# Weight conversions in halves over the steps of the first block, and two copies moved to VectorE

## The chip, the cores and the metric

The kernel runs on one core of one Trainium2 chip. The metric is device microseconds of one launch. Before the change it takes 2700.61 us, the median of 8 runs (2700.15 to 2704.35). A core has five engines that run side by side, each through its own list in order: TensorE (PE; its weight loads are listed as PEld), VectorE (DVE), ScalarE (ACT), GpSimd (POOL) and SyncE (SP), which here issues most DMAs. They wait for each other by semaphores.

## The reference

For 8 sequences of 3008 tokens with 256 channels, a Fourier mixing along the tokens and then a feed-forward layer with hard-swish:

```python
X = np.fft.rfft(x, axis=1)
Y = X * (filt_r + 1j * filt_i)[None]
y = np.fft.irfft(Y, n=3008, axis=1)        # (8, 3008, 256) -> (24064, 256)
h = y @ w_in                               # 256 -> 2048
g = h * np.clip(h + 3.0, 0.0, 6.0) / 6.0
return g @ w_out                           # 2048 -> 256
```

`setup_inputs()` generates the two weights as float64, so the kernel reads them as pairs of 32-bit words and makes float32 of them by itself.

## The kernel before, in words

**Blocks and steps.** The 24064 tokens are 47 blocks of 512. Each block goes through 8 steps, one for each 256 of the 2048 hidden channels; step i of the whole kernel is block i // 8, part p = i % 8. In a step PE multiplies by `w_in[p]` (up), ACT and DVE apply hard-swish, and PE multiplies the step before's result by `w_out[p-1]` (down). The Fourier stages of the following sequence are laid between these products. The order of all instructions is written out by hand: `at(step, function, ...)` puts a call into a plan, the loop over `items` (L925) emits it, and every engine works through its instructions in this order. Within a step, calls of `a_unit`, `b_unit`, `bi_unit` and `n_unit` (the tuple EARLY) come ahead of the down products, all others at the step's end, in the order in which they were planned.

**The first block.** Steps 0 to 7 are block 0, which uses plain products: `plain_up(p)` (L653) writes two PSUM tiles, `al` and `be`, by two matmuls each (L658); `relu` on ACT (L616) and `hswish` on DVE (L621) read each of them and write `g`; `plain_down(p)` (L662, matmuls L669), emitted in step p+1, multiplies `g` by `w_out[p]`. There is one `al` and one `be`, so `plain_up(p+1)` can write them only when `hswish(p)` has read them. Steps from 8 on are block 1 and later: they use seven products in place of eight (`up_1` to `up_5`, L571; `g_sums`; `down`, L647). `plain_down(7)` falls into step 8.

**The conversions.** The weights come in 16 parts of 512 KB: part 2p is `w_in[p]`, part 2p+1 is `w_out[p]`. `w_load` (L260) brings the words of one part into a `bits`, `g` or `xt` tile by a DMA on SP; parts 6, 7 and 10 to 15 share two `bits` tiles, so that part i+2's load waits until part i's words are read. `load_bits` issues the loads that are due. `w_abs` (L266, ACT) takes the upper words' absolute value; `w_conv` (DVE) makes the float32 values by seven instructions: L275, L277, L279, L281, L288, L290, and L293, which writes the whole part into `w_all`, the tile with all weights. Parts 0 to 3 are converted ahead of step 0, parts 4 to 15 in steps 0 to 6 by `convert_one` (one, then two in each of steps 1 to 5, then one), at the end of the step, behind that step's two `hswish` on DVE.

**Sums of weights.** The seven products need sums of the weights' quarters. `w_sums` (L299, POOL) makes three early ones for a part (`late` False) and one late one, which overwrites a quarter and so must come after block 0 has used the part. They are planned from step 6 on; those of parts 14 and 15 begin at step 6.

**First stage of sequence 1.** `a_unit(1, c)`, c = 0 to 7 in steps 2 to 9, transforms slices of `x`: 16 matmuls into two PSUM tiles `psf` (L385), which two ACT copies (L388) bring into the tile `t`; `z_store` sends it to memory on SP's queue. For later sequences there is one copy, and `a_sums` (L394, L395) does the rest on DVE.

**Around it.** `t_sums` (L564, POOL) makes the differences of the activations that the seven products need; `plain_out` (L676, ACT) copies block 0's result out.

Of the kernel before, what the change touches and what calls it, by code (L numbers as in the profile page):

```python
# [38 lines left out]
NB = HC // XC  # L39
# [6 lines left out]
NP = DFF // 256  # L46
# [90 lines left out]
def kernel(  # L137
# [9 lines left out]
    nc = tc.nc  # L147
# [47 lines left out]
    st = {}  # L195
# [38 lines left out]
    def w_part(i):  # L234
        p = i // 2
        if i % 2 == 0:
            cols = ts(p, 256)
            src = moe_w_in[:, cols].bitcast(I32)
            return src.rearrange("(a p) d -> p a d", p=P), w_in[p][:, 0:4, :].rearrange("p (a j) m -> p a (j m)", a=2)
        src = moe_w_out[ts(p, 2 * P), :].bitcast(I32)  # L240
        return src.rearrange("(a p) d -> p a d", p=P), w_out[p][:, 0:4, :].rearrange("p (a j) m -> p a (j m)", a=2)
# [21 lines left out]
    def w_abs(i):  # L263
        words = st["bits", i].rearrange("p (n two) -> p n two", two=2)
        st["high", i] = sp.tile([P, 512], FP32, name="s1")
        nc.scalar.activation(out=st["high", i], in_=words[:, :, 1].bitcast(FP32), func=AXT.Abs)  # L266


    def w_conv(i):
        words = st.pop(("bits", i)).rearrange("p (n two) -> p n two", two=2)  # L270
        lo, hi = words[:, :, 0], words[:, :, 1]
        big, rest = (yp.tile([P, 2, D], FP32, name="y").bitcast(I32).rearrange("p a n -> p (a n)") for j in range(2))
        v = nc.vector
        high = st.pop(("high", i), None)
        v.tensor_scalar(out=big, in0=hi, scalar1=3, scalar2=0x3FFFFFFF,  # L275
                        op0=ALU.logical_shift_left, op1=ALU.bitwise_and)
        v.scalar_tensor_tensor(out=big, in0=hi, scalar=top_c, in1=big,  # L277
                               op0=ALU.bitwise_and, op1=ALU.bitwise_or)
        v.tensor_scalar(out=rest, in0=big, scalar1=23, scalar2=23,  # L279
                        op0=ALU.logical_shift_right, op1=ALU.logical_shift_left)  # L280
        v.tensor_scalar(out=lo, in0=lo, scalar1=9, scalar2=0x3F800000,  # L281
                        op0=ALU.logical_shift_right, op1=ALU.bitwise_or)
        if high is None:
            v.tensor_scalar(out=hi, in0=hi, scalar1=1, scalar2=1,
                            op0=ALU.logical_shift_left, op1=ALU.logical_shift_right)
            high = hi.bitcast(FP32)
        rest, big = rest.bitcast(FP32), big.bitcast(FP32)
        v.scalar_tensor_tensor(out=rest, in0=lo.bitcast(FP32), scalar=1.0, in1=rest,  # L288
                               op0=ALU.subtract, op1=ALU.mult)
        v.scalar_tensor_tensor(out=rest, in0=rest, scalar=2.0 ** -20, in1=big, op0=ALU.mult, op1=ALU.add)  # L290

        two = lambda t: t.rearrange("p (a d) -> p a d", a=2)
        v.scalar_tensor_tensor(out=w_part(i)[1], in0=two(high), scalar=1.125 * 2.0 ** -15, in1=two(rest),  # L293
                               op0=ALU.is_ge, op1=ALU.mult)
# [74 lines left out]
    def bank(b):  # L369
        if b:  # L370
            return psF.tile([P, 512], FP32, name="psf", tag="f")
        st["bank"] = i = (st.get("bank", -1) + 1) % 4
        return psO.tile([P, 2, 2, P], FP32, name="po%d" % i).rearrange("p a u m -> p (a u m)")
# [4 lines left out]
    def a_unit(b, c):  # L378
        xc = xs[:, (b * NB + c) % 3, :, :]
        t = t1p.tile([P, XC // 2, 2, D], FP32, name="t1")  # L380
        ps = [bank(b).rearrange("p (j d) -> p j d", d=D) for h in range(2)]
        for j in range(2):
            for g in range(2):
                for h in range(2):
                    nc.tensor.matmul(ps[h][ts(g, 64), j, :], wa[ds(h * 64, NA), ds((c * XC + 2 * g + j) * 2 * KH, 64)],  # L385
                                     xc[ds(h * 64, NA), 2 * g + j, :], start=True, stop=True)
        for h in range(2 if b == 1 else 1):
            nc.scalar.activation(out=t[:, :, h, :], in_=ps[h], func=AXT.Copy)  # L388
        st["t1", b, c] = t, ps[1]


    def a_sums(b, c):
        t, ps = st["t1", b, c]
        nc.vector.tensor_tensor(out=t[:, :, 1, :], in0=t[:, :, 0, :], in1=ps, op=ALU.subtract)  # L394
        nc.vector.tensor_tensor(out=t[:, :, 0, :], in0=t[:, :, 0, :], in1=ps, op=ALU.add)  # L395

# [100 lines left out]
    for b in range(B):  # L497
        j = 0
        while j < HC:
            n = 1 if b == 0 and j == NJ else min(NJ, HC - j)  # L500
# [229 lines left out]


    EARLY = (a_unit, b_unit, bi_unit, n_unit)

    def at(step, fn, *a):
        plan.setdefault((step, fn in EARLY), []).append((fn, a))

    with tc.manual_schedule():
# [16 lines left out]
        def load_bits(most):  # L754
            nonlocal loaded
            while loaded < most and w_before(loaded) < done:
                w_load(loaded, nc.sync)
                loaded += 1

        def convert(n):  # L760
            nonlocal done
            for i in range(n):
                w_conv(done)
                done += 1


        def convert_one():
            nonlocal done
            w_abs(done)
            w_conv(done)  # L770
            done += 1
            load_bits(NCONV)

# [2 lines left out]
        ps = psU.tile([P, 512], FP32, name="al")  # L776
# [12 lines left out]
        for j in range(0, HC, 4):  # L789
            a0_unit(j)  # L790
            keep_warm({4: 2, 12: 2, 20: 1}.get(j, 0))
            convert(j == 4)
# [34 lines left out]
        for c in range(2):  # L827
            x_load(1, c)
            load_bits(7 + c)
        w_abs(3)  # L830
        convert(3)

        def wai_load():
# [3 lines left out]
        at(0, bi_unit, 0, NU - 2)  # L837
        at(0, g_store, 0, NU - 2)

        for i, s in enumerate((0, 1, 1, 2, 2, 3, 3, 4, 4, 5, 5, 6)):  # L840
            at(s, convert_one)

        for i in range(2):
            at(6, w_sums, 2 * NP - 2 + i, False)
        for p in range(NP):
            for i in range(2):
                if p < NP - 1:
                    at(p + 6, w_sums, 2 * p + i, False)
                at(p + 6, w_sums, 2 * p + i, True)

        at(0, wai_load)
        at(2, x_load, 1, 2)
# [31 lines left out]
        def places(n):  # L884
            if n == 1:
                return (list(range(2, NB + 2)), [12, 13, 15, 18, 19, 20, 22, 23, 26, 27, 28, 30],
                        [14, 15, 16, 19, 21, 22, 24, 25, 27, 29, 30, 31], [16, 21, 24, 29, 31, 32])
            k = first[n] * NP
            a_at = [k - 7 * NP + i for i in (2, 4, 7, 9, 11, 13, 14, 15)]
            f_at, y_at, bi_at = ([k - (5 - 2 * r) * NP + i for r in range(2) for i in p]  # L890
                                 for p in ((2, 3, 6, 7, 12, 13), (4, 5, 10, 11, 14, 15), (8, 14, 17)))
            return a_at, f_at, y_at, bi_at

        prev = None
        for n in range(1, B):
            a_at, f_at, y_at, bi_at = places(n)
            for c, s in enumerate(a_at):
                at(s, a_unit, n, c)
                if n > 1:
                    at(s, a_sums, n, c)  # L900
                at(s, z_store, n, c, nc.sync if n == 1 else nc.gpsimd)
                if c >= 3:
                    at(max(a_at[c - 3], s - 6), x_load, n, c)
                elif n > 1:
                    at(max(prev[c + NB - 3], s - 6), x_load, n, c)
            for c in range(NT):
                s = f_at[2 * (c - TB) + (n == 1)] + 1 if c >= TB else a_at[-1] + 1
                at(s, t2_load, n, c)
                s = f_at[2 * (c - FB) + 1] + 1 if c >= FB else a_at[-1 if n > 1 else 3] + 1
                at(s, table_load, n, c)  # L910
            for i in range(NU):
                if i % 2 == 0 or n == 1:
                    at(f_at[i], b_unit, n, i)
                if i % 2 == 0:
                    at(bi_at[i // 2], bi_unit, n, i)
                    at(bi_at[i // 2], g_store, n, i)
                at(y_at[i], y_unit, n, i)
            for i in range(NU):
                at(f_at[i], f_unit, n, i)
            prev = a_at  # L920
# [4 lines left out]
        for i in range(len(items) + 1):  # L925
            up = i < len(items)
            k, p = items[min(i, len(items) - 1)]
# [54 lines left out]
        k, v, add = NBLK - 1, nc.vector.tensor_tensor, ALU.add  # L982
# [37 lines left out]
```

## Time and profile before

| | |
|---|---|
| median of 8 runs | 2700.61 us |
| profiled execution | 2700.89 us |
| its span, first to last instruction | 2699.1 us |
| first `plain_up` on PE (step 0) | 67.85 us |
| start of step 8 (block 1) on PE | 135.54 us |
| last matmul's end | 2688.07 us |

Times in the trace are microseconds from the span's start. In a line of an engine's work in order of time stand: start, length, engine, line of the kernel, operation, output <- inputs, shapes, the number of instructions run together, and in brackets the idle time of the engine just before with what ended it. Adjacent instructions of an engine overlap by some hundredths to tenths of a microsecond, so I take differences of starts where a chain is summed. A line of the waits holds who waited for whom, the total, how often, and the longest. A line of a stretch holds its bounds and length, busy time and number of instructions of PE, PEld, DVE, ACT and POOL, the granted clock of TensorE (1.00 is full), the DMA share and GB/s.

### The profile page before, as it was taken

The page shows a single profiled execution, that of the slowest core. Times are in us where ns is not written, and L with a number is a line of the kernel's source. Part 1 is how long each engine was busy: PE and PEld are TensorE (multiplying, and loading weights), DVE is VectorE, ACT ScalarE, POOL GpSimd, SP SyncE. Part 2 cuts the span into 40 slices and gives each one's busy share as a digit, 9 for nine tenths or more (in the row PEclk, how much of TensorE's full clock was granted, in tenths as well). Part 3 has the DMA queues.
Part 4 walks back from the last instruction along what each step waited for, and adds up shares of the span by engine and source line. Part 5 has one row for each costly group of instructions (what it writes and reads, how often), then busy time and mean ns, then how long its engine had stood idle before and what let it go on. Part 6 is the DMA issues. An engine that isn't in the chain of part 4 may idle for free.

```text
span 2699.1 us, 48891 instructions
## 1 busy us (share of the span) xinstructions
PE 2675.2 (99%) x18846; PEld 2365.8 (88%) x18846; DVE 2020.5 (75%) x3503; ACT 1306.4 (48%) x2614; POOL 365.7 (14%) x598
## 2 busy tenths in 40 slices
PE   8999999999999999999999999999999999999998
PEld 6588898888988889888888888988888888899997
DVE  7968867787677776787767877677776778766665
ACT  3444444445444444454544545445444454445443
POOL 2141011001210012101121011211112111000000
PEclk9999999999999999999999999999999999999999
DMA  8732133211332113311133111331123321110000
GB/s 236 218 94 71 46 89 99 69 35 42 92 99 63 35 47 95 99 55 37 47 97 96 55 39 52 89 96 55 39 55 89 94 59 36 42 31 18 18 9 17
DMA packets 106598, 185.89 MB, mean 69 GB/s; under 512 B 23609, under 2 KB 66297, under 8 KB 106049
## 3 DMA queue, kind: packets, MB, share of 16 engines
q1 hardware_dynamic: 88607, 138.05, 18.3%
q0 software_dynamic: 17152, 44.22, 6.2%
q8 instruction: 149, 2.44, 0.4%
q14 instruction: 84, 0.69, 0.1%
q10 hardware_dynamic: 606, 0.49, 0.1%
HBM read 110.74 MB, written 71.93 MB: 68 GB/s over the span
## 4 chain that ended last, share of the span: by engine, by line
PE 96%; DVE 2%; DMA 1%; issue 0%; ACT 0%; POOL 0%; POOLq 0%; DVEq 0%; SPq 0%
PE po L647 43%; PE al L571 24%; PE be L571 18%; PE psn L525 4%; PE psf L472 2%; PE psf L385 2%; PE psf L428 1%; PE po L437 0%; PE po L352 0%; PE psf L437 0%; DVE g L621 0%; DVE y L277 0%; DVE y L288 0%; DVE w_all L293 0%; DVE y L290 0%; PE po L669 0%
## 5 line engine op out<-in xcount | busy, mean ns | idle before, releaser
L647 PEld LDWEIGHTS po<-w_all,g 128*128 128x128 f32 x10304 | 1363.3, 191 | 149.3 <-issue 41.4
L647 PE MATMUL po<-w_all,g 128*128 128x128 f32 x10304 | 1403.1, 276 | 0.6 <-DVE g L621 0.6
L616 ACT ACTIVATE r<-h,half_c 128x512 f32<-128x512 f32 x736 | 531.1, 722 | 328.9 <-DVE h L597 316.9
L621 DVE SCALAR_TENSOR_TENSOR g<-r,h 128x512 f32<-128x512 f32 x736 | 508.0, 690 | 206.3 <-ACT r L616 191.6
L571 PE MATMUL al<-xt,w_all 128*128 128x256 f32 x2208 | 660.0, 381 | 1.2 <-DVE h L602 0.6
L571 PE MATMUL be<-xn,w_all 128*128 128x256 f32 x1472 | 437.8, 379 | 0.0
L597 DVE TENSOR_TENSOR h<-be,s 128x512 f32<-128x512 f32 x368 | 254.3, 691 | 219.6 <-PE be L571 208.4
L571 PEld LDWEIGHTS al<-xt,w_all 128*128 128x128 f32 x2208 | 335.3, 192 | 2.5 <-DVE h L602 1.2
L571 PEld LDWEIGHTS be<-xn,w_all 128*128 128x128 f32 x1472 | 279.7, 190 | 37.9
L611 ACT ACTIVATE h<-al 128x256 f32<-128x256 f32 x368 | 141.0, 383 | 343.9 <-PE al L571 343.9
L602 DVE TENSOR_TENSOR h<-al,s 128x256 f32<-128x256 f32 x368 | 156.2, 424 | 166.7 <-PE al L571 165.6
L629 DVE TENSOR_TENSOR g<-g 128x512 f32<-128x512 f32 x368 | 256.1, 696 | 12.6
L592 ACT ACTIVATE s<-al 128x256 f32<-128x256 f32 x368 | 141.2, 384 | 205.7 <-PE al L571 203.6
L583 ACT ACTIVATE s<-be 128x256 f32<-128x256 f32 x368 | 141.1, 383 | 176.7 <-PE be L571 176.7
L571 PE MATMUL al<-xn,w_all 128*128 128x256 f32 x736 | 219.9, 381 | 0.5 <-ACT h L611 0.5
L571 PE MATMUL be<-xt,w_all 128*128 128x256 f32 x736 | 218.9, 379 | 0.0
L631 DVE TENSOR_TENSOR g<-g 128x256 f32<-128x256 f32 x368 | 169.9, 462 | 12.5
L582 ACT ACTIVATE s<-al 128x256 f32<-128x256 f32 x368 | 141.0, 383 | 71.3 <-PE al L571 71.3
L628 DVE TENSOR_TENSOR g<-g 128x256 f32<-128x256 f32 x368 | 157.3, 427 | 12.6
L571 PEld LDWEIGHTS be<-xt,w_all 128*128 128x128 f32 x736 | 139.8, 190 | 18.9
L402 POOL DMA_DIRECT2D z_tmp<-t x192 | 95.2, 502 | 417.4 <-DVE t L395 399.1
L492 POOL DMA_DIRECT2D g_tmp<-t x84 | 52.7, 632 | 584.3 <-ACT t L475 584.3
(139 smaller groups left out, 1812.0 us busy)
## 6 DMA issues: line engine op xcount, KB each, us to landing
g_tmp<-t POOLq DMA_DIRECT2D x96, 256.0 KB, 3.7
t<-g_tmp SPq DMA_DIRECT2D x188, 120.0 KB
t<-z_tmp SPq DMA_DIRECT2D x42, 512.0 KB
z_tmp<-t POOLq DMA_DIRECT2D x192, 96.0 KB, 3.4
out_dram<-o SPq DMA_DIRECT2D x321, 47.0 KB
xs<-in_x_dram SPq DMA_DIRECT2D x112, 128.0 KB
ft<-in_filt_r_dram SPq DMA_DIRECT2D x168, 64.0 KB
ft<-in_filt_i_dram SPq DMA_DIRECT2D x168, 64.0 KB
```

Of the source, the lines that this page charges most:

```text
L571: nc.tensor.matmul(ps, w_in[p][:, w, :], x, start=start, stop=stop, skip_group_check=True)
L582: nc.scalar.activation(out=s[:, 0, :], in_=al, func=AXT.Copy)
L583: nc.scalar.activation(out=s5, in_=be[:, 1, :], func=AXT.Copy)
L592: nc.scalar.activation(out=s[:, 1, :], in_=al, func=AXT.Copy)
L597: nc.vector.tensor_tensor(out=st["h"][0].rearrange("p (a n) -> p a n", a=2), in0=be, in1=s, op=ALU.add)
L602: nc.vector.tensor_tensor(out=st["h"][1][:, 256:512], in0=al, in1=s5, op=ALU.add)
L616: nc.scalar.activation(out=r, in_=st["h"][i], func=AXT.Relu, bias=half_c, scale=1.0 / 6.0)
L621: nc.vector.scalar_tensor_tensor(out=st["g", k, p][:, o:o + 2, :].rearrange("p a n -> p (a n)"), in0=st["r", i], scalar=1.0, in1=st["h"][i ...
L628: v.tensor_tensor(out=g[:, G1, :], in0=g[:, G3, :], in1=g[:, G22, :], op=ALU.add)
L629: v.tensor_tensor(out=g[:, G3:G2 + 1:2, :], in0=g[:, G3:G1 + 1, :], in1=g[:, G11:G11 + 1, :].broadcast_to([P, 2, 256]), op=ALU.subtract)
L631: v.tensor_tensor(out=g[:, G4, :], in0=g[:, G12, :], in1=g[:, G2, :], op=ALU.subtract)
L647: nc.tensor.matmul(st["po", k][bank][:, part, u, :], g[:, a, ts(u, P)], w_out[p][:, w, :], start=(p == 0 and n in OPENS and u == 0), stop= ...
```

## The change

`w_conv` is split: the first four instructions stay in it, the last three (L288 to L293) become `w_conv_2`. `convert_one` becomes `convert_half`, called alternately for the first half (with `w_abs` ahead of it) and the second (with `load_bits` behind it). 24 halves are planned over steps 0 to 7, three in each of steps 0 to 5, four in step 6 and two in step 7. On POOL, part 14's early sums stay first in step 6, part 15's move to step 13, and part 14's late one to the end of step 13. For c = 6 and 7 (steps 8 and 9) `a_unit(1, c)` leaves the second tile's copy to `a_sums`, which makes it on DVE at the end of the step.

```diff
@@ w_conv
-        high = st.pop(("high", i), None)
+        st["conv", i] = big, rest, lo, hi
         v.tensor_scalar(out=big, in0=hi, scalar1=3, scalar2=0x3FFFFFFF,
...
         v.tensor_scalar(out=lo, in0=lo, scalar1=9, scalar2=0x3F800000,
                         op0=ALU.logical_shift_right, op1=ALU.bitwise_or)
+
+    def w_conv_2(i):
+        big, rest, lo, hi = st.pop(("conv", i))
+        v = nc.vector
+        high = st.pop(("high", i), None)
...
@@ a_unit, a_sums
-        for h in range(2 if b == 1 else 1):
+        for h in range(2 if b == 1 and c < NB - 2 else 1):
             nc.scalar.activation(out=t[:, :, h, :], in_=ps[h], func=AXT.Copy)
...
         t, ps = st["t1", b, c]
+        if b == 1:
+            if c >= NB - 2:
+                nc.vector.tensor_copy(out=t[:, :, 1, :], in_=ps)
+            return
...
-        def convert_one():
+        def convert_half(second):
             nonlocal done
-            w_abs(done)
-            w_conv(done)
+            if not second:
+                w_abs(done)
+                w_conv(done)
+                return
+            w_conv_2(done)
             done += 1
             load_bits(NCONV)
...
-        for i, s in enumerate((0, 1, 1, 2, 2, 3, 3, 4, 4, 5, 5, 6)):
-            at(s, convert_one)
-
-        for i in range(2):
-            at(6, w_sums, 2 * NP - 2 + i, False)
-        for p in range(NP):
-            for i in range(2):
-                if p < NP - 1:
-                    at(p + 6, w_sums, 2 * p + i, False)
-                at(p + 6, w_sums, 2 * p + i, True)
+        half = 0
+        for s, n in enumerate((3, 3, 3, 3, 3, 3, 4, 2)):
+            for i in range(n):
+                at(s, convert_half, half % 2)
+                half += 1
+
+        order = [2 * NP - 2] + [i for i in range(2 * NP) if i != 2 * NP - 2]
+        for i in order:
+            at((6 + i // 2) if i != order[0] else 6, w_sums, i, False)
+            if i != order[0]:
+                at(6 + i // 2, w_sums, i, True)
+        at(6 + NP - 1, w_sums, order[0], True)
...
                 at(s, a_unit, n, c)
-                if n > 1:
-                    at(s, a_sums, n, c)
+                at(s, a_sums, n, c)
```

The other conversions, parts 0 to 3, call both halves one after the other. No other line changes.

More of the change, by code (lines that the diff above doesn't have):

```diff
@@ L763, in convert @@
                 w_conv(done)
+                w_conv_2(done)
                 done += 1
-        def convert_one():
+        def convert_half(second):
             nonlocal done
-            w_abs(done)
-            w_conv(done)
+            if not second:
+                w_abs(done)
+                w_conv(done)
+                return
+            w_conv_2(done)
             done += 1
```

## The prediction

> **What bounds the kernel now.** I read the page's busy shares first, then PE's waits, then PE, DVE and ACT in order of time around the change.
>
> ```profile
> span 2699.1 us, 48891 instructions
> PE 2675.2 (99%) x18846; PEld 2365.8 (88%) x18846; DVE 2020.5 (75%) x3503; ACT 1306.4 (48%) x2614; POOL 365.7 (14%) x598
> ```
>
> PE is busy 99% of the span: 23.9 us are all that any reordering can win, and a delay of PE anywhere is not made good later. The profiled execution took 2700.89 us, its span and 1.8 us around it; the median of the eight runs is 2700.61, 0.3 lower. I sum against 2700.89. Next, PE's waits from 60 to 260 us, where the changed steps lie:
>
> ```profile
> PE al L658 <- DVE g L621: 3.0, 3, 1.3
> ...
> PE al L571 <- ACT s L592: 0.5, 1, 0.5
> ```
>
> The three waits of L658 (`plain_up`) lie in the first block; in PE's order of time they are:
>
> ```profile
> 108.15 1.98 PE L658 MATMUL al<-xn,w_all 128*128 128x512 f32 x4 [0.57 <-DVE g L621]
> ...
> 117.69 1.98 PE L658 MATMUL al<-xn,w_all 128*128 128x512 f32 x4 [1.17 <-DVE g L621]
> ...
> 127.33 1.98 PE L658 MATMUL al<-xn,w_all 128*128 128x512 f32 x4 [1.26 <-DVE g L621]
> ```
>
> These are the starts of steps 5, 6 and 7. Each waits for the `hswish` of the step before, which must read `al` before PE writes it again. DVE does it late, since two conversions of the step before stand ahead of it. DVE at the last of them:
>
> ```profile
> 122.32 0.42 DVE L275 TENSOR_SCALAR y<-bits 128x512 int32<-128x512 int32 x1
> ...
> 125.98 0.69 DVE L293 SCALAR_TENSOR_TENSOR w_all<-s,y 128x512 f32<-128x512 f32 x1 [0.20 <-DVE y L290]
> 126.59 0.68 DVE L621 SCALAR_TENSOR_TENSOR g<-r,al 128x512 f32<-128x512 f32 x1
> 127.19 0.68 DVE L621 SCALAR_TENSOR_TENSOR g<-r,be 128x512 f32<-128x512 f32 x1
> ```
>
> The conversion that ends at 126.67 is number 14, the weight `w_in[7]` that `plain_up(7)` reads at 127.33. So now the weight is ready 0.66 us before it is wanted, and `hswish(6)`, queued behind it, is what ends last. From 72.3 to 133 us DVE has no idle time but 0.2 us: the chain is DVE work back to back.
>
> **The change, part by part.** What is wanted when: `plain_up(p)` in step p reads part 2p; `plain_down(p)` in step p+1 reads part 2p+1. Write A for the first half of a conversion (four instructions), B for the second (three). Before, steps 0 to 6 convert 4 | 5 6 | 7 8 | 9 10 | 11 12 | 13 14 | 15. After, steps 0 to 7 hold 4A 4B 5A | 5B 6A 6B | 7A 7B 8A | 8B 9A 9B | 10A 10B 11A | 11B 12A 12B | 13A 13B 14A 14B | 15A 15B. Within a step DVE's order stays: two `hswish`, then conversions. Thus part 10 moves from step 3 to 4, part 12 from step 4 to 5, part 14 from step 5 to 6: each is now converted in the step just before it is read, **behind** that step's `hswish`, which waits for PE's own `plain_up`. That closes a loop that was open: PE's `plain_up(6)`, relu, `hswish(6)`, four halves, PE's `plain_up(7)`.
>
> Durations, from step 0 of the trace:
>
> ```profile
> 72.30 0.69 DVE L621 SCALAR_TENSOR_TENSOR g<-r,be 128x512 f32<-128x512 f32 x1 [0.96 <-ACT r L616]
> 72.91 0.42 DVE L275 TENSOR_SCALAR y<-xt 128x512 int32<-128x512 int32 x1
> ...
> 74.96 0.69 DVE L288 SCALAR_TENSOR_TENSOR y<-xt,y 128x512 f32<-128x512 f32 x1
> ...
> 76.48 0.69 DVE L293 SCALAR_TENSOR_TENSOR w_all<-s,y 128x512 f32<-128x512 f32 x1
> 77.09 0.68 DVE L621 SCALAR_TENSOR_TENSOR g<-r,al 128x512 f32<-128x512 f32 x1
> ```
>
> A = 74.96 - 72.91 = 2.05. B = 77.09 - 74.96 = 2.13; until PE may use its result 1.52 + 0.74 = 2.26 (L293 starts 1.52 into B; DVE's L621 started at 126.59 and PE went at 127.33, 0.74 later). Two `hswish` 1.20 (77.09 to the next L275 at 78.29). `plain_up(0)` began at 67.85 and DVE was through its `hswish` at 72.91: a loop through PE, ACT and DVE of 5.06 before the first half can start. PE's own step, unstalled: 8.10 (step 2, 79.49 to 87.59), 9.92 (step 3), 10.07 (step 4 less its 0.57), 8.21 (step 7, 127.33 to 135.54); I use 8.2 for steps 5 and 6.
>
> The sum, with U for the start of `plain_up`:
> - Step 0: 72.91 + A+B+A 6.23 = 79.14. `hswish(1)` frees `al` 0.75 later: U2 = 79.89 (79.49 now), a new wait of 0.4.
> - Step 1: 79.14 + 1.20 + 6.31 = 86.65, as now. U3 = 79.89 + 8.10 = 87.99; part 6 and `hswish(2)` (87.4) are in time.
> - Step 2 ends at 86.65 + 1.20 + 6.23 = 94.08; U4 = 87.99 + 9.92 = 97.91. Part 8 ends at 94.08 + 1.20 + 2.26 = 97.54, just in time.
> - Step 3 ends at 95.28 + 6.31 = 101.59. POOL's four subtractions at 94.9 to 105.4 (L564) stretch DVE's instructions beside them now: L293 at 95.57 took 1.03 for 0.69, and part 10 from L275 to L290 took 4.12 (101.89 to 106.01) where part 4 took 2.78 (72.91 to 75.69), 1.34 more. They will fall on step 3, to 101.93, and on step 4, which begins its halves at 103.13.
> - Part 10 ends for PE at 103.13 + 2.05 + 2.26 + 1.3 = **U5 = 108.74** (now 108.15; PE alone would be there at 107.98). The stretch is the unsure term: without it U5 is 107.98, 0.8 less; I keep 1.3, for the same four POOL instructions run.
> - U5 + 5.06 = 113.80; 11B 12A 12B then take 2.13 + 2.05 + 2.26: **U6 = 120.24** (now 117.69). PE is done with step 5 at 116.94 and idles 3.3.
> - U6 + 5.06 = 125.30; 13A 13B 14A 14B take 8.49: **U7 = 133.79** (now 127.33). PE is done with step 6 at 128.44 and idles 5.35.
> - Step 8 begins at 133.79 + 8.21 = 142.00 for 135.54 now: **+6.46**.
>
> The waits that go (0.57, 1.17, 1.26) are inside this difference. Part 15 moves to step 7: 133.79 + 5.06 + 4.31 = 143.2, with POOL's sums beside it up to 2.7 more if each of seven instructions is stretched by about 0.4, as above. `plain_down(7)` wants it 4.6 into step 8 (140.13 - 135.54), 146.6 or 146.05 with the saving below: hidden, by 0.1 in the worst case.
>
> The two copies: in step 8 ACT's two L388 (1.08 together) stand ahead of L592, for which PE waits 0.5 at 139.63. One moves to DVE, behind `hswish(0)` at 141.7, where DVE is then idle until 145.45: **-0.5** at best, 0 if part 15 eats it; I take -0.35. In step 9 PE doesn't wait for ACT there, and DVE has 0.7 free after L621 at 150.51. Both tiles leave on SP, which is at output stores from 142.68 to 155.09, so a later copy costs nothing; without that cover step 9's copy would make its store 3 us later.
>
> The bits loads: 12 to 15 are issued a step later, each when the tile's former part is read. Part 14's load goes when 12B's L288 is done, about 118.7, and lands some 4.5 later (115.58 to ACT's 120.06 now), 123.2, against 14A at 129.5: hidden. On SP the stores and loads of the first stage stand behind them by up to 8 us; their readers are two steps away. POOL: part 14's sums wait for part 14, ready just before U7; they and the eight of step 6 after them (0.54 each, 43 in 23.10 us) take 6, and step 8 wants the first of these 8.2 on. The sums of 15 go behind `t_sums(2)`, 3 instructions of 0.54: POOL is through near 185, and step 15 begins near 195.
>
> **The clock.** A gap of 5.35 us in PE is longer than any between its first and last matmul now (1.49 at 64.61). What such a gap costs is seen only at the ends. The last matmuls, and two stretches behind them (PE, PEld, DVE, ACT, POOL busy, then granted clock):
>
> ```profile
> 2685.13 2.94 PE L647 MATMUL po<-w_all,g 128*128 128x128 f32 x24 [0.62 <-DVE g L621]
> ```
> ```profile
> 2690.00:2692.00 2.00, 0.00 (x0) 0.00 (x0) 0.25 (x1) 0.00 (x0) 2.00 (x5) 1.00 0.38 107
> 2692.00:2693.00 1.00, 0.00 (x0) 0.00 (x0) 0.00 (x0) 0.00 (x0) 1.00 (x3) 0.63 0.50 139
> ```
>
> PE ended at 2688.07; 0.63 in a microsecond between 1.00 and 0.50 puts the fall at 2692.26, 4.2 later. And at the start:
>
> ```profile
> 2.89 3.50 PE L780 MATMUL al<-r 128*128 128x512 f32 x4 [2.89 <-ACT r L774]
> ...
> 10.00 1.88 PE L780 MATMUL al<-r 128*128 128x512 f32 x4
> ```
>
> The first four take 3.50, the same four later 1.88: a cold start costs 1.6. If the clock falls in the gap before U7, `plain_up(7)` is slow by about that. Bounds: 0 and 1.6 (3.2 if it stays slow twice as long). The one row says that 5.35 is enough, by 1.1 us; as one row can't fix the moment, I take half, **+0.8**.
>
> [...]
>
> Sum: 6.46 - 0.35 + 0.8 = 6.9; 2700.89 + 6.9 = **2707.8 us**.
>
> **Rivals.**
> 1. *Forecast: parts 12 and 14 are late.* 84%. Ends: no POOL stretch (-0.8), full saving (-0.15), no fall of the clock (-0.8): 2706.0; clock slow twice as long (+2.4) and no saving (+0.35): 2710.5. With 0.5 below for the scatter of the runs (2700.15 to 2700.82 but for one): 2705.5 to 2710.5.
> 2. *The evening out works.* Halves spread DVE's work, 7.4 us in a step against PE's 8.2, so `hswish` comes in time and the waits at steps 5 to 7 and the 0.5 go: -3.5, 2697.4, not slower. The place is U7. It decides if PE finds part 14 ready at U6 + 8.2, that is if a half takes no more than (8.2 - 5.06 - 0.13)/4 = 0.75 us; the rows have 2.09. For it speaks that the sums per step fit; against it, that step 6 holds four halves, and their start hangs on `plain_up(6)`. 3%.
> 3. *Only part of the lateness arrives.* The loop through relu is shorter than 5.06, or PE's lead at step 5 larger, and U7 moves by 1 to 5: 2702 to 2705.5. For it: steps 0 to 4 lie within 0.6 us of now. Against: from U5 on every term is a row. 8%.
> 4. *More is late.* The clock falls in both gaps, or part 15 under POOL's sums holds up `plain_down(7)`: 2710.5 to 2714. The gap at step 6 is 3.3, under 4.2. 5%.
>
> **How the numbers follow.** Range 2704.5 to 2711: cases 1, much of 4's lower end and the top of 3. Slower by over 0.2% (above 2706.0; about what a measurement of this kernel can tell from no change): nine tenths of case 1 and all of 4, 0.81. Within 0.2%: the rest of 1, cases 3 and 2 (-3.5 is 0.13%), 0.18. Faster by over 0.2% would need 5.4 us where PE's waits hold 4: 0.01.
>
> **What would show it.** PE waits for `plain_up` in the first block named by `w_all` (the last instruction of a conversion) and no longer by `g`: about 0.8, 3.3 and 5.4 us before steps 5, 6 and 7; the start of step 8 near 142; the 0.5 for ACT's L592 gone; a granted clock under 1 in the microsecond around 133 where the clock fell; from step 9 on the same order 6 us later. I am wrong if DVE runs without idle time from step 4 to step 6, for then the loop isn't closed, or if a later wait of PE shrinks by what was lost.

## The result, and the profile after

The changed kernel takes 2711.02 us, the median of 10 runs (2709.57 to 2712.39); the kernel before, run beside it, 2700.83. The ratio is 1.0036 with a 95% interval of 1.0028 to 1.0045: **slower by 10 us**. The profiled execution took 2710.27 us, 9.4 more than that of before. The forecast was slower, 2707.8; the median lies at the upper end of its range, 0.02 us above 2711.0.

The page of the profile after, span and busy shares:

```profile
span 2708.5 us, 48886 instructions
PE 2678.5 (99%) x18846; PEld 2366.9 (87%) x18846; DVE 2023.5 (75%) x3505; ACT 1308.0 (48%) x2612; POOL 368.3 (14%) x598
```

The work is the same; the span is 9.4 us longer, and PE's busy time 3.3 us: so PE stood idle for 6.1 us more, and its matmuls took 3.3 us more. PE's waits over the whole span (by the added lines `plain_up`, L658 before, is now L667, `hswish`, L621 before, is L630, and the last instruction of a conversion, L293 before, is L298):

```profile
PE al L667 <- DVE w_all L298: 9.0, 3, 5.3
```

Before, the same matmuls waited 3.0 us for `g`; now they wait 9.0 us for `w_all`, the weight itself. PE in order of time:

```profile
108.75 1.98 PE L667 MATMUL al<-xn,w_all 128*128 128x512 f32 x4 [0.68 <-DVE w_all L298]
...
120.18 1.98 PE L667 MATMUL al<-xn,w_all 128*128 128x512 f32 x4 [3.05 <-DVE w_all L298]
...
133.84 3.78 PE L667 MATMUL al<-xn,w_all 128*128 128x512 f32 x4 [5.29 <-DVE w_all L298]
137.42 2.90 PE L667 MATMUL be<-xn,w_all 128*128 128x512 f32 x4
...
144.83 0.59 PE L580 MATMUL al<-xn,w_all 128*128 128x256 f32 x2
...
148.51 0.67 PE L580 MATMUL al<-xt,w_all 128*128 128x256 f32 x2
```

`plain_up(5)`, `(6)` and `(7)` begin at 108.75, 120.18 and 133.84; the last begins with the same four matmuls as the others, but they take 3.78 for 1.98. Step 8 begins at 144.83 for 135.54 before. At 148.51 stands the product that waited 0.55 for ACT before (139.63): the wait is gone. Why the weight is late is seen on DVE:

```profile
119.43 0.69 DVE L298 SCALAR_TENSOR_TENSOR w_all<-s,y 128x512 f32<-128x512 f32 x1
122.92 0.69 DVE L630 SCALAR_TENSOR_TENSOR g<-r,al 128x512 f32<-128x512 f32 x1 [2.80 <-ACT r L625]
124.64 0.69 DVE L630 SCALAR_TENSOR_TENSOR g<-r,be 128x512 f32<-128x512 f32 x1 [1.03 <-ACT r L625]
125.24 0.44 DVE L275 TENSOR_SCALAR y<-bits 128x512 int32<-128x512 int32 x1
...
133.10 0.69 DVE L298 SCALAR_TENSOR_TENSOR w_all<-s,y 128x512 f32<-128x512 f32 x1 [0.20 <-DMA bits<-in_moe_w_out_dram]
```

This is the loop, closed: part 12 is done at 120.1, PE may start `plain_up(6)`; DVE, which before never paused here, waits 3.8 us for PE and ACT; then it converts 13 and 14, and PE waits 5.29 us for DVE. The engines take turns. And the clock, in stretches (PE, PEld, DVE, ACT, POOL busy; granted clock, DMA share, GB/s):

```profile
130.00:133.00 3.00, 0.00 (x0) 0.00 (x0) 2.79 (x5) 0.00 (x0) 0.00 (x0) 0.94 0.79 272
133.00:134.00 1.00, 0.16 (x1) 0.16 (x1) 0.69 (x1) 0.00 (x0) 0.08 (x1) 0.50 0.63 250
...
139.00:140.00 1.00, 1.00 (x3) 0.34 (x1) 0.07 (x1) 0.00 (x0) 0.92 (x3) 0.77 0.48 135
```

It falls to 0.50 in the gap, at 132.64 (finer stretches put it there), and is back at 139.47. From 133.84 to 139.47 PE works at a granted clock of 0.50, 5.63 us, of which half, 2.8, is lost.

The shift of PE's instructions against before, matmul by matmul: 0.12 from the first `plain_up` on, 0.39 at step 2, 0.60 at step 5, 2.49 at 6, 6.51 at 7, 9.29 at 8, 8.88 from 148.51 to 600 us, and 9.03 at the last matmul. All of it but 0.15 us arises in the first block and step 8, and nothing later takes any of it back; the span's other 0.3 us lie behind the last matmul.

### The profile page after: what moved, and what is told of

Read it like the earlier page. It is cut to its first block, busy times and chain, and to the rows that moved or that the text cites. A ratio compares the mean times of both kernels' runs of the same rounds, so it can differ in the third digit from the quotient of the medians.

```text
span 2708.5 us, 48886 instructions
## 1 busy us (share of the span) xinstructions
PE 2678.5 (99%) x18846; PEld 2366.9 (87%) x18846; DVE 2023.5 (75%) x3505; ACT 1308.0 (48%) x2612; POOL 368.3 (14%) x598
## 4 chain that ended last, share of the span: by engine, by line
PE 95%; DVE 2%; DMA 1%; SPq 0%; issue 0%; ACT 0%; POOL 0%; POOLq 0%; DVEq 0%
PE po L656 43%; PE al L580 24%; PE be L580 18%; PE psn L534 4%; PE psf L481 2%; PE psf L390 2%; PE psf L437 1%; DMA w_all<-in_x_dram 0%; PE psf L446 0%; PE al L667 0%; PE po L446 0%; DVE g L630 0%; PE be L667 0%; DVE y L277 0%; DMA wa<-wb_t 0%; DVE w_all L298 0%
## 5 line engine op out<-in xcount | busy, mean ns | idle before, releaser
L630 DVE SCALAR_TENSOR_TENSOR g<-r,h 128x512 f32<-128x512 f32 x736 | 508.0, 690 | 205.8 <-ACT r L625 191.5
L592 ACT ACTIVATE s<-be 128x256 f32<-128x256 f32 x368 | 141.4, 384 | 176.3 <-PE be L580 176.3
```

The source lines that it names most:

```text
L592: nc.scalar.activation(out=s5, in_=be[:, 1, :], func=AXT.Copy)
L630: nc.vector.scalar_tensor_tensor(out=st["g", k, p][:, o:o + 2, :].rearrange("p a n -> p (a n)"), in0=st["r", i], scalar=1.0, in1=st["h"][i ...
```

## The experiments

The theory: two losses, the delay of parts 12 and 14 (6.4 us by the trace, less 0.4 from the copies), and falls of the clock in the gaps that the delay makes. Rivals: `plain_up(7)` is slow because of GpSimd's sums or the loads beside it; the copies or the reordered sums cost; or DVE is simply full, whatever the order. In the table, the time is a median, the ratio is to the kernel before on the same chip; "fall" and "back" are the moments of the clock in the profile, from half-microsecond stretches.

| run | us | ratio (95%) | fall, back (profiled execution) |
|---|---|---|---|
| changed | 2711.02 | 1.0036 (1.0028 to 1.0045) | 132.64, 139.47 |
| e1_fill8 | 2710.12 | 1.0037 (1.0023 to 1.0051) | 119.33, 122.74 |
| f1_fill_both | 2708.89 | 1.0030 (1.0019 to 1.0040) | 134.03, 137.44 |
| f2_fill_7 | 2709.25 | 1.0028 (1.0017 to 1.0040) | none |
| f5_fill_2_2 | 2709.43 | 1.0030 (1.0018 to 1.0041) | 132.73, 139.55 |
| g1_fill_more | 2707.36 | 1.0023 (1.0014 to 1.0033) | none |
| e5_343 | 2707.92 | 1.0023 (1.0014 to 1.0032) | 132.57, 135.98 |
| f3_halves_only | 2712.02 | 1.0045 (1.0031 to 1.0058) | 118.69, 125.51 and 135.75, 139.17 |
| e2_copies | 2700.40 | 0.9997 (0.9989 to 1.0006) | none |
| g2_before_steps | 2700.63 | 1.0001 (0.9992 to 1.0010) | none |
| e4_order | 2698.01 | 0.9991 (0.9982 to 1.0) | none |
| g3_order_again | 2698.72 | 0.9994 (0.9985 to 1.0003) | none |

**Filling the gaps.** All five runs of this kind add to the changed kernel, with other numbers for steps 6 and 7:

```diff
             if k == 0:
+                if p in {6: 2, 7: 4}:
+                    fill = psU.tile([P, 512], FP32, name="al")
+                    for j in range({6: 2, 7: 4}[p]):
+                        nc.tensor.matmul(fill, w_in[p - 1][:, 0, :], xb(0, 0), start=True, stop=True)
                 plain_up(p)
```

e1_fill8, eight ahead of `plain_up(7)`:

> The changed kernel with eight extra matmuls of 0.43 us each (w_in[6] times a slice of xn into al, overwritten at once by plain_up(7)) ahead of plain_up(7), in the gap in which PE waits for part 14. Theory (the late part 14 is one loss, the fall of the clock in the 5.3 us gap another): the gap shrinks to about 1.9 us, plain_up(7) still starts near 133.8, the granted clock stays 1.00 there, plain_up(7) takes 3.5 us instead of 6.4 and step 8 starts near 142.0 instead of 144.8; the whole falls by 2.8 to about 2707.5 in a profile and by 3 to 4.5 in the median, as the changed kernel's runs (2709.6 to 2712.4) must all hold a fall. Rival (plain_up(7) is slow for another reason, the 43 sums on GpSimd or the filter loads that run beside it): it stays at 6.4 us and the time stays at 2711.

It missed, and told something by it. PE, and a stretch beside `plain_up(7)`:

```profile
119.48 3.59 PE L667 MATMUL al<-xn,w_all 128*128 128x512 f32 x4 [3.05 <-DVE w_all L298]
...
129.29 7.03 PE L952 MATMUL al<-xn,w_all 128*128 128x512 f32 x16
136.38 1.98 PE L667 MATMUL al<-xn,w_all 128*128 128x512 f32 x4
```
```profile
136.00:138.00 2.00, 1.94 (x5) 0.87 (x5) 0.00 (x0) 0.00 (x0) 1.84 (x5) 1.00 0.71 151
```

An extra matmul takes 0.88 us, not 0.43, so eight (7.03) overran the gap and held up `plain_up(7)` until 136.38. There it took 3.63 us with the clock at 1.00, though the sums and loads ran beside it as before (GpSimd busy for 1.84 of 2 us and a DMA share of 0.71; in the changed kernel, from 136 to 137 us, 0.92 of 1 us and 0.70): the first part of the theory holds, that rival falls. But now the clock fell in the **other** gap, of 3.05 us, ahead of `plain_up(6)`, at 119.33. I had thought that gap too short.

f1_fill_both, two and four:

> The changed kernel with extra matmuls into al (overwritten at once) in both gaps: two ahead of plain_up(6), four ahead of plain_up(7). In the run with eight, one of them took 0.88 us, so the gaps shrink from 3.05 to 1.3 and from 5.3 to 1.8. Theory (a fall of the clock needs a gap of at least about two microseconds of idle PE; what is left is the delay of the conversions alone): plain_up(7) starts at 133.8, its step takes 8.2, the granted clock is 1.00 throughout, step 8 starts at 142.0; 2700.9 + 6.5 - 0.4 = 2707.0 and nearly all runs there. Rival (plain_up(7) is slowed by GpSimd's sums or the loads beside it): about 2710, as the changed kernel.

Three of the seven runs came out at 2706.8 to 2707.7, as expected; the others did not. The profiled one (2708.89), PE and then the clock:

```profile
120.00 1.96 PE L667 MATMUL al<-xn,w_all 128*128 128x512 f32 x4 [1.43 <-DVE w_all L298]
...
133.72 3.45 PE L667 MATMUL al<-xn,w_all 128*128 128x512 f32 x4 [1.95 <-DVE w_all L298]
```
```profile
133.00:134.00 1.00, 0.28 (x1) 0.30 (x2) 0.57 (x1) 0.00 (x0) 0.29 (x1) 1.00 0.53 209
134.00:135.00 1.00, 1.00 (x2) 0.33 (x1) 0.00 (x0) 0.00 (x0) 0.84 (x3) 0.51 0.69 157
```

A gap of 1.95 us was enough, and the clock fell at 134.03, when PE was at work again. The "about two microseconds" of the expectation were an estimate of mine: they lie between the gap of 1.49 us at 64.61 in the kernel before, where the clock stays at 1.00, and the 3.05 of e1_fill8.

f2_fill_7, four ahead of `plain_up(7)` alone:

> The changed kernel with the four extra matmuls ahead of plain_up(7) only; the gap of 3.05 us ahead of plain_up(6) stays. [...]

Without a fall this kernel would take some 2707.0, the sum of f1_fill_both; a fall as long as that of e1_fill8 (3.41 us at 0.50) adds 1.7 by my estimate, 2708.7. Its profile shows no fall in a gap of 3.05 us and one of 1.95 (granted clock 1.00 from 114 to 144 us), and that execution, 2707.52, is the shortest of six; the others are at 2708.8 to 2712.2. So, by these times, the same gaps are caught (the clock falls for them) in one run and not in the next; what decides it is not shown. By the times five of six runs are caught, and not at one level.

f5_fill_2_2, two in either gap:

> The changed kernel with two extra matmuls in either gap: 1.3 us of idle PE are left ahead of plain_up(6) and 3.55 ahead of plain_up(7). [...]

All six runs lie at 2708.4 to 2710.2, none at 2707: by these times a gap of 3.66 us (by its trace) is caught every time. In the profile the clock fell at 132.73, when PE had stood still for only 2.5 us (since 130.21).

g1_fill_more, three and five:

> The changed kernel with three extra matmuls ahead of plain_up(6) and five ahead of plain_up(7) (0.88 us each, into al, overwritten at once): gaps of about 0.5 and 1.0 in place of 1.4 and 1.95. [...] Rival (falls come from something else than the idle time): runs scattered from 2707 to 2712 as with two and four.

Eight of nine runs lie within 2706.5 to 2708.6, near the 2707.0 without a fall; the rival's scatter up to 2712 is not seen. The waits and the clock in its profile, which lies 1.2 us later than that of the changed kernel from the first `plain_up` on (69.17 for 67.97):

```profile
121.46 1.96 PE L667 MATMUL al<-xn,w_all 128*128 128x512 f32 x4 [0.57 <-DVE w_all L298]
...
135.18 1.96 PE L667 MATMUL al<-xn,w_all 128*128 128x512 f32 x4 [1.09 <-DVE w_all L298]
```
```profile
132.00:138.00 6.00, 4.91 (x12) 1.99 (x11) 2.87 (x6) 0.69 (x1) 2.52 (x6) 1.00 0.81 227
```

Eight matmuls more, for nothing, and the kernel is 3.7 us **faster** than the changed one (2711.02 to 2707.36). The kernel before took 2700.83 beside the one and 2700.79 beside the other. This is the two losses apart: 2707.36 - 2700.79 = 6.6 us for the delay, and 3.7 us in the median for the clock. By this trace step 8 begins 74.20 us after the first `plain_up`, for 67.69 before: the delay is 6.5 us, and 6.1 with the 0.4 of the copies.

**Where the halves stand.** e5_343 and g2_before_steps change one line of the changed kernel:

```diff
-        for s, n in enumerate((3, 3, 3, 3, 3, 3, 4, 2)):
+        for s, n in enumerate((3, 3, 3, 3, 3, 4, 3, 2)):     # e5_343
+        for s, n in enumerate((2, 4, 4, 4, 4, 4, 2)):        # g2_before_steps
```

> The changed kernel with one half moved: 3, 3, 3, 3, 3, 4, 3, 2, order of the parts as it was; part 13A runs in step 5, while DVE waits for PE, and step 6 holds three halves. Theory: plain_up(6) at 120.2 as in the changed kernel, plain_up(7) at 120.2 + 5.06 + 6.44 = 131.7 in place of 133.8, a gap of 3.2 us in place of 5.3. [...] Rival (the clock falls in gaps of 3.2 us too): plain_up(7) takes 5 us or more, 2706.5 or more.

`plain_up(7)` began at 131.67, as worked out to 0.03 us; the loop's price by halves holds. But the clock fell here too:

```profile
131.67 2.92 PE L667 MATMUL al<-xn,w_all 128*128 128x512 f32 x4 [3.21 <-DVE w_all L298]
134.38 2.68 PE L667 MATMUL be<-xn,w_all 128*128 128x512 f32 x4
```
```profile
131.00:132.00 1.00, 0.33 (x1) 0.30 (x2) 0.61 (x1) 0.00 (x0) 0.26 (x1) 1.00 0.81 324
132.00:133.00 1.00, 1.00 (x3) 0.51 (x2) 0.00 (x0) 0.00 (x0) 0.84 (x3) 0.79 0.59 193
```

PE stood still until 131.67, and the clock went down at 132.57, 0.9 us after. Without a fall step 8 would begin near 139.9 (131.7 + 8.2), 4.4 later than before; with 0.4 less for the copies that makes some 2704.8. The shortest of the eleven runs is 2706.51, 1.7 over that estimate. The rival was right here.

> The changed kernel with halves 2, 4, 4, 4, 4, 4, 2: the conversions stand in the steps where the kernel before has them, and all else is as changed (split functions, order of the sums on GpSimd, two copies on DVE). Theory (the whole loss is where the halves stand): step 8 at 135.5, 0.4 saved in step 8 by the copies, 2700.4. Rival (the later sums of part 15 or the copies cost something): 2701.5 or more.

2700.63, ratio 1.0001 (0.9992 to 1.0010). With the halves in the steps of before, `plain_up(7)` waits 1.27 for `g` again, and the split, the order of the sums and the copies cost nothing that can be measured. The interval alone leaves room for 2.7 us; the trace is closer: step 8 begins 67.68 us after the first `plain_up`, for 67.69 before and 76.86 in the changed kernel. The 0.4 of the copies can't be told from none in these medians.

**The copies.** e2_copies is the kernel before with the edits of `a_unit`, `a_sums` and the loop at L899; f3_halves_only is the changed kernel without them:

```diff
-        for h in range(2 if b == 1 else 1):
+        for h in range(2 if b == 1 and c < NB - 2 else 1):
...
+        if b == 1:
+            if c >= NB - 2:
+                nc.vector.tensor_copy(out=t[:, :, 1, :], in_=ps)
+            return
```

> The kernel before with only the two copies of steps 8 and 9 moved to DVE; conversions as before. Theory: PE's 0.55 us wait for ACT's L592 in step 8 goes to about 0.1, nothing else moves: 2700.4, 0.4 under before. Rival (the later copies delay z_store or PSUM tiles): a wait of PE for psf or for the first b_unit appears, 2701 to 2704.

> The changed kernel without the two copies on DVE (both copies of a_unit on ACT in steps 8 and 9, as before); conversions in halves as changed. Theory: PE's wait of 0.5 for L592 in step 8 is back, 0.4 more than the changed kernel: 2711.4, step 8 at 144.8 as there or, where the clock falls otherwise, within 1.7 of it. Rival (the copies are a part of the loss): under 2710.

e2_copies gives 2700.40 and no new wait; its interval takes in 1. The product that waited for ACT begins 3.68 us into step 8, for 4.09 before. In the trace of f3_halves_only the wait for ACT (L592 before, L597 here) is back:

```profile
119.44 3.78 PE L663 MATMUL al<-xn,w_all 128*128 128x512 f32 x4 [3.05 <-DVE w_all L298]
...
136.10 3.49 PE L663 MATMUL al<-xn,w_all 128*128 128x512 f32 x4 [5.29 <-DVE w_all L298]
...
149.86 0.67 PE L576 MATMUL al<-xt,w_all 128*128 128x256 f32 x2 [0.50 <-ACT s L597]
```

Here the clock fell in both gaps, and both `plain_up` are slow. The copies are no part of the loss; the traces give them 0.4.

**Another order.** e4_order keeps the halves and converts, of two neighbours, the part of `w_in` first (g3_order_again is the same kernel):

```diff
+    ORD = (0, 1, 2, 3, 4, 6, 5, 8, 7, 10, 9, 12, 11, 14, 13, 15)
+
     def w_part(i):
+        i = ORD[i]
         p = i // 2
...
-        for s, n in enumerate((3, 3, 3, 3, 3, 3, 4, 2)):
+        for s, n in enumerate((3, 3, 3, 3, 3, 4, 3, 2)):
```

> The changed kernel with halves 3, 3, 3, 3, 3, 4, 3, 2 and with the parts converted in the order 4 6 5 8 7 10 9 12 11 14 13 15, so that each part of w_in comes one conversion earlier and the part of w_out, wanted 4.5 us later in the step, after it. Theory (the loss is the loop relu, hswish, halves, next plain_up): only the second half of parts 12 and 14 stands between hswish and the next plain_up, 5.06 + 2.26 = 7.3 us, less than PE's step of 8.2, so steps 5 and 6 start without a wait, step 7 near 124.9 with a wait of 0.5 or less, step 8 near 133.1 (before 135.5); clock at 1.00; total 2.9 under before, 2698. Rival (DVE is full, so that any order is as late as before): step 8 at 135.5 or later, 2700.5 or more.

> The reordered kernel (parts 4 6 5 8 7 10 9 12 11 14 13 15, halves 3 3 3 3 3 4 3 2) once more, for a firmer interval: 2698.0, 2.9 under before, step 8 near 133; faster than before by 0.1%.

PE of e4_order:

```profile
116.00 1.88 PE L670 MATMUL al<-xn,w_all 128*128 128x512 f32 x4
...
124.44 1.98 PE L670 MATMUL al<-xn,w_all 128*128 128x512 f32 x4 [0.17 <-DVE w_all L301]
...
129.42 3.72 PE L681 MATMUL po<-w_all,g 128*128 128x256 f32 x16 [0.25 <-DVE w_all L301]
```

The waits of steps 5 and 6 are gone, step 7 begins at 124.44 with a wait of 0.17 (worked out: 124.9, at most 0.5), and step 8 at 132.98 (worked out: 133.1) for 135.54 before. The 0.25 us for which `plain_down` waits in step 7 were not foreseen. The span is 2696.1, 3.0 under before; the medians are 2698.01 and 2698.72 (before: 2701.05 and 2700.79). The intervals, up to 1.0 and 1.0003, don't clear one: some runs of either kernel lie about 3.5 us above the rest with a lower mean clock (0.997, for 0.998 to 0.999), 13 of the 65 of before that ran beside these experiments and eight of 22 here. No profile caught such a run; where their clock falls stays open. So the order is shown to take the waits away, and its gain of 2 to 3 us is not shown beyond the noise.

## Why the prediction was right or wrong, point by point

| term | forecast | measured |
|---|---|---|
| start of `plain_up(5)` | 108.74 | 108.75 |
| start of `plain_up(6)`, gap | 120.24, 3.3 | 120.18, 3.05 |
| start of `plain_up(7)`, gap | 133.79, 5.35 | 133.84, 5.29 |
| GpSimd's stretch of DVE in step 4 | 1.3 | 1.47 (L277 to L281: 1.29, 0.83, 0.95 for 0.75, 0.43, 0.42, beside POOL's L573 at 103.43 to 106.16) |
| copies | -0.35 | -0.41 (shift 9.29 to 8.88) |
| fall of the clock | +0.8, at most 1.6 (3.2) | +2.8 in the profile, 3.7 in the median |
| part 15 ahead of `plain_down(7)` | hidden | hidden: done at 147.0, wanted at 149.0 |
| total | +6.9 | +9.4 in the profile, +10.2 in the medians |

**The chain was right.** The reason, the place and the price of the delay came out to 0.1 us, since each term was a row of the trace and the chain had one order only. Rivals 2 and 3 didn't come about: a half takes 2.1 us where 0.75 would have been needed. g2_before_steps shows that the place of the halves is all of the loss, and g1_fill_more that the delay alone, copies included, is worth 6.1 by its trace and 6.6 by its median (forecast 6.1).

The median lies in the band of rival 4 (2710.5 to 2714), but neither of its two conditions is seen in the changed kernel's profile: the clock fell in one gap, and part 15 held up nothing. That execution, 2710.27, lies near the upper end of the forecast's own case (2710.5), a clock that stays slow twice as long. Falls in both gaps, as in the profile of f3_halves_only, could be what brings the median's 3.7 us above the profile's 2.8; no profile of the changed kernel shows them.

**The step that failed is the clock.** "As one row can't fix the moment, I take half, +0.8", and "the gap at step 6 is 3.3, under 4.2". The 4.2 us of that row were taken for a fixed delay behind PE's last matmul; in the changed kernel the same row gives 2.4 (last matmul's end 2697.10, fall 2699.47). In the gaps the falls came 4.1 (changed), 4.1 (e5_343), 2.9 (e1_fill8), 2.5 (f5_fill_2_2) and 2.3 us (f1_fill_both) after PE had stopped, in e5_343 and f1_fill_both with PE at work again. So the gap of 3.05 counts as well, and the one of 5.29 is, by the times, caught in every run: the shortest run of the changed kernel is 2.2 us over g1_fill_more's median. The price was low too: I took the 1.6 us of the start for the likely size, though in the trace of before the granted clock reads 1.00 there (from 2 to 6 us), so that this row shows no fall and no price of one; and the clock stayed down for 6.83 us in the changed kernel's profile, the "twice as long" that I had only as an end of the range.

## What to carry to other kernels

Work spread more evenly over the steps of a loop can still end up on the wrong side of a wait: here DVE had room for its share in every step but step 6, and still the last of the weight was made behind an instruction that waits for the very matmul before the one that needs it. So ask of each moved instruction not only how full its engine is, but what stands ahead of it in the queue and what that waits for; and order the work by when it is wanted within the step. Here the new gaps on PE (3.05 and 5.29 us in the changed kernel) cost their length, and, in the executions in which the clock fell, half of the time that PE then worked with the clock at 0.50 (2.8 us in the profile of the changed kernel).

## What the runs showed of the hardware

**The granted clock beside PE's gaps in the first block.** Every gap ahead of `plain_up(6)` and `plain_up(7)` that `w_all` ended, in the profiles of the changed kernel and of the runs with its order of conversions:

| run, gap ahead of | gap, us | clock falls at (after PE stopped) | back at | down for, us |
|---|---|---|---|---|
| changed, `plain_up(7)` | 5.29 | 132.64 (4.1) | 139.47 | 6.83 |
| f3_halves_only, `plain_up(7)` | 5.29 | 135.75 (4.9) | 139.17 | 3.42 |
| f5_fill_2_2, `plain_up(7)` | 3.66 | 132.73 (2.5) | 139.55 | 6.82 |
| e5_343, `plain_up(7)` | 3.21 | 132.57 (4.1) | 135.98 | 3.41 |
| e1_fill8, `plain_up(6)` | 3.05 | 119.33 (2.9) | 122.74 | 3.41 |
| f3_halves_only, `plain_up(6)` | 3.05 | 118.69 (2.3) | 125.51 | 6.82 |
| changed, e5_343, f2_fill_7, `plain_up(6)` | 3.05 | none | | |
| f1_fill_both, `plain_up(7)` | 1.95 | 134.03 (2.3) | 137.44 | 3.41 |
| f2_fill_7, `plain_up(7)` | 1.95 | none | | |
| f1_fill_both, f5_fill_2_2, `plain_up(6)` | 1.43, 1.42 | none | | |
| g1_fill_more, `plain_up(6)`, `plain_up(7)` | 0.57, 1.09 | none | | |

While it was down the granted clock read 0.50, and the first four matmuls of a `plain_up` that lay wholly in such a stretch took 3.75 to 3.78 us for 1.98 (changed from 133.84, f5_fill_2_2 from 133.87, f3_halves_only from 119.44). In these profiles the clock fell in each of the four gaps of 3.21 us or more, in two of the five of 3.05, in one of the two of 1.95, and in none of the four of 1.43 or less. So in these profiles the length of the gap alone doesn't say whether the clock falls: gaps of 3.05 and of 1.95 were caught in some and not in others. Nor does the start of the matmul behind it: `plain_up(7)` of e5_343 began at 131.67 at a clock of 1.00, which fell 0.9 us later. What decides between equal gaps, and between 3.4 and 6.8 us down, is not shown.
